# The first batch's attention rows: kept in SBUF and turned around by the tensor engine, in place of a store to DRAM and gathers

## The chip, the cores and the metric

The kernel runs on one core of one Trainium2 chip. The metric is the device time of one launch in microseconds (us). The kernel before took 1281.42 us, the median of three runs (1279.94 to 1284.14). The host only lays out inputs and puts the output rows back in order.

## The reference

Eight batches of eight heads of block-causal attention (576 positions, head size 64, blocks of 64), then, per batch, the real part of a two-dimensional Fourier transform, a normalization and a feed-forward layer.

```python
scores = scale * np.matmul(q, k.transpose(0, 1, 3, 2))
scores = np.where(block_i >= block_j, scores, -1000000000.0)
attn = softmax(scores)
x = np.matmul(attn, v)           # then (batch, position, 8 heads * 64)
mixed = np.real(fft(fft(x, axis=1), axis=2))
u = x + mixed
un = (u - mean(u)) / np.sqrt(var(u) + 1e-06)
out = u + np.maximum(un @ w_ch1, 0.0) @ w_ch2
```

## The kernel before

`tile_attn_fourier_ffn` writes one instruction stream for the whole launch. Pieces of work are `Step` objects in lanes: loading and preparing a head, the row maxima, the scores, the values, and the Fourier transform of a batch. A second list, `feeds`, holds the feed-forward steps of finished row tiles; they are the filler between attention steps. A third, `sides`, holds the weight loads and their conversion. The loop at line 1068 keeps estimated queues of the engines and picks the next step; `AHEAD` (line 36) says how far a side step may be queued on an engine. Each engine then runs in that order (`Ordered`, `keep_in_program_order`), so a changed step or cost can move instructions on every engine.

Attention, per head: `max_part` (row maxima, "lead" matmuls), `shift`, `scores` (pairs of "rest" and "lead" matmuls, exponentials on ScalarE as `ph` and `p`, the small part `pl` on GpSimd), `values` (45 "av" matmuls). At the end of `values`, VectorE divides: `den`, `rec`, and one multiplication of 128x320 into `x`. After every second head, two SP DMAs store the pair's columns of `x` to the DRAM tile `xd`.

When the last head of a batch is stored, `mirror` (line 603) reads back: 256 lower rows into `LL`, 33 middle rows into `X2` (both by SP), and, in reversed row order, the upper rows into `UU` and `U2` by three indirect GpSimd DMAs with the table `rows`. `folded` (line 625) adds and subtracts lower and upper rows on VectorE ("tmp", then the split "fs"); `stage1` and `stage2` are the Fourier matmuls ("dft"), with split results "zc", "zs", "ZT"; `stage2_cos` makes "dif" and "add" on VectorE and adds them to `u` on GpSimd. `normalized_steps` then makes mean and variance, `un`, its transposition ("ident,un"), and `uh`/`ul`, which open a feed of two row tiles.

A feed has two parts: `first` ("h<-uh,W" and "h<-ul,W", 192 matmuls of 256 columns) and `second` ("acc<-W,gh", "acc<-W,gl", 192 of 512 columns). Feed 1 does all of `first` and then all of `second`. Its weights are made meanwhile: `weight_single` has three VectorE instructions on a 128x1024 tile ("W<-W"), one ScalarE square, then a scale per matrix (`weight_scale`, "wst<-ps") and `weight_parts` on ScalarE, GpSimd and VectorE. `second` waits for the scale of the second matrix.

```python
sync.dma_start(LL, xd[0:256].rearrange("(c p) d -> p c d", p=P))
sync.dma_start(X[2], xd[256:289])
for dst, i in ((U[0], 0), (U[1], 1), (U2[0:32], 2)):
    gpsimd.indirect_dma_start(dst, None, xd, bass.IndirectOffsetOnAxis(ap=rows[0:dst.shape[0], i:i + 1], axis=0))
```

Of the kernel before, what the change touches and what calls it, by code (L numbers as in the profile page):

```python
# [9 lines left out]
F32 = mybir.dt.float32  # L10
# [4 lines left out]
ALU = mybir.AluOpType  # L15
# [4 lines left out]
B, H, S, D = 8, 8, 576, 64  # L20
DM = H * D
FF = 4 * DM
P = 128
# [9 lines left out]

HOP = 0.25
MARGIN = 0.3
AHEAD = (3.0, 6.0)
FREE = 0.5

TABLES = (1, 2, 4, 5)
# [161 lines left out]
def tile_attn_fourier_ffn(  # L201
# [5 lines left out]
    work = pool("work")  # L207
# [4 lines left out]
    def ps_tile():  # L212
        return ps[current].tile([P, 512], F32, name=current)

    def mm(*args, **kw):
        return tc.keep_in_program_order(nc.tensor.matmul(*args, **kw))  # L216
# [4 lines left out]
    vector, scalar, gpsimd, sync = (Ordered(tc, x) for x in (nc.vector, nc.scalar, nc.gpsimd, nc.sync))  # L221


    ident = const.tile([P, P], F32, name="ident")
# [59 lines left out]
    def ready(step):  # L284
        r = max((done[x] for x in step.after), default=0.0)
        return max(r, min(rings[x][0] for x in lent)) if step.bank else r
# [13 lines left out]
    def issue(step):  # L300
        nonlocal current, now
        t = max(now, ready(step))
        if step.cost:
            give(t)
        if step.cost:
            now = t = t + step.cost
            for x in queues.values():
                x.forget(now)
        free = None
        starts = []  # L310
        for engine, cost in step.chain:
            if engine == "B":
                free = t + HOP
            elif engine == "L":
                t = t + cost
            elif engine in scratch:

                if cost:
                    t = max(t, scratch[engine][0] - HOP)
                else:  # L320
                    scratch[engine] = sorted(scratch[engine][1:] + [t + HOP])
            else:
                t = book(engine, t + HOP, cost)
                if engine != "M":
                    starts.append(t - cost)
        t += HOP
        if step.key is not None:
            done[step.key] = t
        if step.bank:
            current = min(lent, key=lambda x: rings[x][0])  # L330
            rings[current] = rings[current][1:] + [t if free is None else free]
        parts = step.emit()
        if parts is None:
            return
        if step.cost:
            next(parts, None)
        for at in starts:
            pending.append((at, len(pending) + 1000000 * issued[0], parts))
        issued[0] += 1
# [179 lines left out]
    xs = {}  # L519
    avs = {}  # L520

    def values(h, at):
        g, hh = divmod(h, 2)
        b, n = divmod(h, H)
        vh, vl = VH[g % 2], VL[g % 2]
        if at == 0:
            avs[h] = ps_av.tile([P, 5, D + 1], F32, name="av")
        av = avs[h]
        c = CHUNKS[at]
        tile_, col = ((0, 0), (1, 0), (2, 0), (2, 320), (1, 448))[c]  # L530
        ph, pl = probs[h, tile_]
        for j in range(c, 5):

            lo = col + P * (j - c) - (64 if j == 4 else 0)
            for i, (lhs, rhs, w) in enumerate((
                (ph, vh[:, c, hh], D + 1), (ph, vl[:, c, hh], D), (pl, vh[:, c, hh], D + 1)
            )):
                mm(
                    av[:, j, 0:w], lhs[:, lo:lo + P], rhs, start=(at == 0 and j == 0 and i == 0),
                    stop=(at == 4 and i == 2), skip_group_check=True,  # L540
                )
        if at < 4:
            return
        yield
        del avs[h]
        if n == 0:
            xs[b] = dram.tile([S, DM], F32, name="xd")
        if hh == 0:
            xs["pair"] = work.tile([P, 5, 2, D], F32, name="x", bufs=1)
        xd, x = xs[b], xs["pair"]  # L550
        den, sc = DEN[h % 2], pairs[g]
        eps = 1e-9 * 2.0 ** PSHIFT
        vector.tensor_scalar(den, av[:, :, D], eps, sc, op0=ALU.add, op1=ALU.mult)
        rec = work.tile([P, 5], F32, name="rec", bufs=2)
        vector.reciprocal(rec, den)
        vector.tensor_tensor(
            x[:, :, hh], av[:, :, 0:D], rec.unsqueeze(2).to_broadcast([P, 5, D]), op=ALU.mult
        )
        yield
        if hh == 1:  # L560
            ds = slice(D * (n - 1), D * (n + 1))
            sync.dma_start(
                xd[0:512, ds].rearrange("(c p) d -> p c d", p=P), x[:, 0:4].rearrange("p c h d -> p c (h d)")
            )
            sync.dma_start(xd[512:576, ds], x[64:128, 4].rearrange("p h d -> p (h d)"))
            yield
# [20 lines left out]
    def value_lane():  # L587
        for h in range(B * H):
            for n, c in enumerate(CHUNKS):
                yield Step(  # L590
                    lambda n=n: values(h, n), 0.09 * (5 - c), ("D0.95",) + (("Q1.2",) if h % 2 else ()) if n == 4 else (),
                    (("S", h, (0, 1, 1, 2, 2)[n]), ("N", h // 2)) + ((("V", h - 1, 4),) if h else ()) + ((("d", h // H - 3, "u"),) if n == 4 and h >= 3 * H else ()),
                    ("V", h, n), place=h + 0.5,
                )


    def utile():
        return work.tile([P, 2, DM], F32, name="u", bufs=5)

    def fourier_steps(b):  # L600
        U, X, low, up = [], [], [], []

        def mirror():
            xd = xs.pop(b)
            LL, UU = utile(), utile()
            U.extend((UU[:, 0], UU[:, 1], work.tile([97, DM], F32, name="U2", bufs=1)))
            X.extend((LL[:, 0], LL[:, 1], work.tile([33, DM], F32, name="X2", bufs=1)))
            low.extend(X[0:2])
            up.extend(U[0:2])
            if b % 2 == 0:  # L610
                lefts.append(work.tile([P, DM], F32, name="left", bufs=2))
            U2 = U[2]
# [3 lines that stand above are left out]
                gpsimd.indirect_dma_start(  # L616
                    dst, None, xd, bass.IndirectOffsetOnAxis(ap=rows[0:dst.shape[0], i:i + 1], axis=0)
                )
            gpsimd.memset(U[0][0:1], 0.0)
            gpsimd.memset(U2[32:33], 0.0)  # L620
            yield
# [90 lines left out]
        def stage2_cos(c):  # L712
# [27 lines left out]

        D_ = lambda *a: ("d", b) + a
        place = H * (b + 0.9)
        yield Step(
            mirror, 0.0, ("P3", "L2.5"), (("V", H * b + H - 1, 4),) + ((("F", feed_number(b - 2, 1)),) if b > 1 else ()), D_("u"),
            place=place,
        )
        def folds(name, op, width):
            for c in (2, 0, 1):
                yield Step(
                    lambda c=c: folded(op, width, name, c), 0.0, ("t1",) + (("X1.6", "A1.2", "X0.9") if c == 2 else ("X1.12", "A0.41", "X0.43")) + ("t",), (D_("u"),),  # L750
                    D_("f" + name) if c == 1 else None, place=place,
                )
# [14 lines left out]
        for c in (2, 0, 1):  # L767
# [3 lines left out]
                place=place,  # L771
# [9 lines left out]
    lefts = []  # L781
# [48 lines left out]
    def feed_number(b, i):  # L830

        return 2 * b + 1 + b // 4 if i == 2 else 2 * b + 1 + (b + 1) // 4 + i
# [227 lines left out]
    def transform_lane():  # L1060
        for b in range(B):
            yield from fourier_steps(b)

    lanes = [table_lane(), head_lane(), prepare_lane(), v_lane(), max_lane(), score_lane(), value_lane(), transform_lane()]
    heads = [next(x) for x in lanes]
    weights, filler = [load_lane(), *(weight_lane(w) for w in range(2))], None
    sides = [next(x) for x in weights]
    while True:
# [13 lines left out]
        for w, side in enumerate(sides):  # L1082
# [86 lines left out]
```

## Time and profile before

| | |
|---|---|
| median of three runs | 1281.42 us (1279.94 to 1284.14) |
| the profiled execution's own time | 1277.07 us |
| its span, first to last instruction | 1275.3 us |
| mean granted TensorE clock | 0.947 of full speed |
| busy share: PE, VectorE, ScalarE, GpSimd | 93%, 55%, 43%, 41% |

The span is what the trace covers; some 1.8 us of the execution lie outside it. PE is TensorE's matmul queue, PEld its weight loads, DVE is VectorE, ACT ScalarE, POOL GpSimd, and SP the queue that issues most DMAs. A busy share is a mean over stages: this kernel has an opening stage without filler and a long stage with it, and they have to be read apart.

### The profile page before, as it was taken

Reading aid. Unit: us, or ns where it says so; the run is one execution under the profiler, and the core shown is the slowest. Engines: PE = TensorE matmul, PEld = TensorE weight load, DVE = VectorE, ACT = ScalarE, POOL = GpSimd, SP = SyncE. Lnnn points to the kernel's source line nnn. Section 1 sums busy time; section 2 is a strip of 40 time slices with the busy share of each in tenths; the row PEclk is TensorE's granted clock in tenths of the full one; section 3 lists DMA queues with packets and bytes.
Section 4 is the critical chain, followed back from the end, with each engine's and each line's share of the span. In section 5 each row is a group of like instructions: output and inputs, shape, how many; then the busy total and the mean of one; then the engine's idle time right before and its main releaser. Section 6 shows DMA issues by size and latency. Waiting matters only on the chain.

```text
span 1275.3 us, 25121 instructions
## 1 busy us (share of the span) xinstructions
PE 1181.1 (93%) x10068; PEld 892.9 (70%) x10068; DVE 703.5 (55%) x1433; ACT 548.7 (43%) x1137; POOL 523.6 (41%) x593
## 2 busy tenths in 40 slices
PE   5772598999799999999999999999999999999998
PEld 5672376677677777777777777777777667766665
DVE  6787777756747574664546573557445414422211
ACT  5655647554444555534645545454443112111110
POOL 4664944454643654563534644446441400300000
PEclk9655688999899999999999999999999999999999
DMA  7674242342223233232323232413220100000000
GB/s 210 201 243 156 80 140 70 87 111 52 74 71 109 62 81 86 79 75 54 93 75 95 65 90 68 111 51 87 77 74 10 40 19 19 21 17 1 17 17 17
DMA packets 56371, 99.07 MB, mean 78 GB/s; under 512 B 7757, under 2 KB 26653, under 8 KB 56256
## 3 DMA queue, kind: packets, MB, share of 16 engines
q1 hardware_dynamic: 49152, 73.16, 21.2%
q10 hardware_dynamic: 4384, 16.78, 4.0%
q0 software_dynamic: 2720, 7.54, 2.1%
q8 instruction: 79, 1.29, 0.4%
q14 instruction: 36, 0.29, 0.1%
HBM read 58.46 MB, written 18.87 MB: 61 GB/s over the span
## 4 chain that ended last, share of the span: by engine, by line
PE 80%; DVE 10%; POOL 3%; issue 3%; DMA 2%; ACT 1%; SPq 0%; DVEq 0%; POOLq 0%; ACTq 0%
PE acc L216 28%; PE h L216 27%; PE ps L216 17%; PE av L216 6%; DVE W L194 2%; DVE M L194 2%; DVE tmp L194 2%; PE ps L219 2%; POOL u L194 1%; DMA lead<-mt 1%; DVE VL L194 1%; POOL W L194 1%; POOL pl L194 1%; DVE rest L194 1%; POOL ag L194 0%
## 5 line engine op out<-in xcount | busy, mean ns | idle before, releaser
L216 PE MATMUL h<-uh,W 128*128 128x256 f16 x2304 | 431.4, 275 | 2.7 <-DVE M L194 2.3
L194 POOL TENSOR_TENSOR pl<-p,ph 128x288 f16<-128x288 f32 (+1 forms) x256 | 253.7, 1002 | 355.6 <-ACT p L194 167.8
L216 PEld LDWEIGHTS <-W 128*128 128x128 f16 x3456 | 325.8, 99 | 64.9 <-issue 6.3
L216 PE MATMUL acc<-W,gh 128*128 128x512 f16 x1104 | 329.8, 380 | 0.0
L216 PE MATMUL h<-ul,W 128*128 128x256 f16 x1152 | 315.8, 274 | 0.0
L194 DVE TENSOR_REDUCE M<-ps 128x1 f32<-128x448 f32 (+3 forms) x292 | 131.9, 484 | 181.3 <-PE ps L216 180.5
L194 ACT ACTIVATE gh<-h 128x512 f16<-128x512 f32 x138 | 82.3, 597 | 305.1 <-PE h L216 302.3
L216 PE MATMUL ps<-lead 72*128 72x64 f32 (+9 forms) x700 | 201.3, 346 | 9.2 <-ACT lead L194 6.8
L216 PE MATMUL acc<-W,gl 128*128 128x512 f16 x552 | 209.2, 379 | 0.0
L194 DVE SCALAR_TENSOR_TENSOR gl<-h,gh 128x512 f16<-128x512 f32 x138 | 94.6, 687 | 200.9 <-ACT gh L194 200.8
L194 ACT ACTIVATE ph<-ps 128x512 f16<-128x512 f32 (+1 forms) x233 | 117.5, 506 | 146.9 <-PE ps L216 144.3
L216 PEld LDWEIGHTS <-gh 128*128 128x128 f16 x1104 | 96.7, 98 | 80.1 <-issue 4.7
L216 PEld LDWEIGHTS ps<-lead 72*128 72x128 f32 (+1 forms) x700 | 128.0, 202 | 18.3 <-ACT lead L194 6.8
L216 PEld LDWEIGHTS <-ph 128*128 128x128 f16 x1920 | 113.5, 104 | 31.1 <-ACT left L194 4.9
L216 PE MATMUL ps<-rest 128*128 128x320 f32 (+3 forms) x350 | 124.0, 361 | 1.4 <-ACT p L194 0.8
L216 PE MATMUL av<-VH,ph 128*128 128x65 f16 x960 | 118.1, 203 | 6.1 <-DVE x L194 6.1
L194 ACT ACTIVATE p<-ps 128x512 f32<-128x512 f32 (+1 forms) x233 | 117.2, 505 | 4.3 <-POOL pl L194 2.8
L216 PE MATMUL av<-VH,pl 128*128 128x65 f16 x960 | 116.6, 201 | 1.8 <-POOL pl L194 1.4
L216 PE MATMUL av<-VL,ph 128*128 128x64 f16 x960 | 117.2, 201 | 0.0
L194 POOL TENSOR_TENSOR rest<-raw,lead 64x576 fp32r<-64x576 f32 x64 | 96.9, 1514 | 15.1 <-ACT lead L194 9.5
L216 PEld LDWEIGHTS <-gl 128*128 128x128 f16 x552 | 54.0, 98 | 66.2 <-DVE gl L194 1.7
L216 PEld LDWEIGHTS <-pl 128*128 128x128 f16 x960 | 94.8, 103 | 2.7 <-POOL pl L194 2.5
(169 smaller groups left out, 1435.4 us busy)
## 6 DMA issues: line engine op xcount, KB each, us to landing
raw<-in_qk_dram SPq DMA_DIRECT2D x64, 288.0 KB
rest<-lead SPq DMA_DIRECT2D x128, 144.0 KB
W<-in_moe_w_ch_dram ACTq DMA_DIRECT2D x14, 1024.0 KB
V<-in_v_dram SPq DMA_DIRECT2D x32, 320.0 KB
xd<-x SPq DMA_DIRECT2D x32, 256.0 KB
out_dram<-u SPq DMA_DIRECT2D x32, 256.0 KB
u<-xd SPq DMA_DIRECT2D x8, 512.0 KB
u<-in_moe_w_ch_dram ACTq DMA_DIRECT2D x4, 512.0 KB
```

Source lines behind the costliest of these rows:

```text
L194: x = f(*args, **kw)
L216: return tc.keep_in_program_order(nc.tensor.matmul(*args, **kw))
L219: return tc.keep_in_program_order(nc.tensor.transpose(*args, **kw))
```

## The change

For batch 0 alone, the rows no longer pass through DRAM. `first_rows` takes the tiles `LL`, `X2`, `UU`, `U2` at head 0 and builds `flip`, a reversed identity with zeros on both sides. The division of each head writes three pieces: chunks 3 and 4 into a slot of `x`, chunk 2 into `X2`, chunks 0 and 1 into `LL`. After each pair of heads, `turned` multiplies with slices of `flip` (five fp32 matmuls into one PSUM bank) and ScalarE copies the result into `UU` and `U2`. `known` only hands the tiles on, at no instruction. The eight stores, two loads, three gathers and two GpSimd memsets of batch 0 are gone. `AHEAD` goes from (3.0, 6.0) to (2.75, 3.0). The other seven batches are as before.

```diff
-AHEAD = (3.0, 6.0)
+AHEAD = (2.75, 3.0)
...
+        if b == 0:
+
+            LL, X2, _, _ = xs[0]
+            hs = slice(D * n, D * (n + 1))
+            at = n // 2 % 2 * 2
+            for dst, lo, hi in ((x[:, at:at + 2, hh], 3, 5), (X2[:, hs].unsqueeze(1), 2, 3), (LL[:, :, hs], 0, 2)):
+                vector.tensor_tensor(
+                    dst, av[:, lo:hi, 0:D], rec[:, lo:hi].unsqueeze(2).to_broadcast([P, hi - lo, D]), op=ALU.mult
+                )
+            yield
+            return
...
+    flip = work.tile([P, DM], F32, name="un", bufs=2)
+    def first_rows():
+        LL, UU = utile(), utile()
+        U2 = work.tile([97, DM], F32, name="U2", bufs=1)
+        X2 = work.tile([P, DM], F32, name="X2", bufs=1)
+        xs[0] = LL, X2, UU, U2
+        vector.memset(flip[:, 0:65], 0.0)
+        vector.memset(flip[:, 193:256], 0.0)
+        vector.tensor_copy(flip[:, 65:193], ident[:, ::-1])
+        vector.memset(U2[32:33], 0.0)
+    def turned(n):
+        LL, X2, UU, U2 = xs[0]
+        x = xs["pair"]
+        ds = slice(2 * D * n, 2 * D * (n + 1))
+        t = ps_tile()
+        at = (slice(0, P), slice(P, 2 * P), slice(2 * P, 3 * P))
+        last = [x[:, n % 2 * 2 + c].rearrange("p h d -> p (h d)") for c in range(2)]
+        mm(t[:, at[0]], flip[:, 0:P], last[0], start=True, stop=False, skip_group_check=True)
+        mm(t[:, at[0]], flip[64:P, 64:64 + P], last[1][64:P], start=False, stop=False, skip_group_check=True)
+        mm(t[:, at[1]], flip[:, P:2 * P], last[0], start=False, stop=False, skip_group_check=True)
+        mm(t[:, at[1]], flip[:, 0:P], X2[:, ds], start=False, stop=False, skip_group_check=True)
+        mm(t[0:32, at[2]], flip[:, P:P + 32], X2[:, ds], start=False, stop=True, skip_group_check=True)
+        yield
+        scalar.copy(UU[:, :, ds], t[:, 0:2 * P].rearrange("p (c x) -> p c x", c=2))
+        scalar.copy(U2[0:32, ds], t[0:32, at[2]])
+        yield
...
-        yield Step(
-            mirror, 0.0, ("P3", "L2.5"), (("V", H * b + H - 1, 4),) + ((("F", feed_number(b - 2, 1)),) if b > 1 else ()), D_("u"),
-            place=place,
-        )
+        if b == 0:
+            for n in range(H // 2):
+                yield Step(
+                    lambda n=n: turned(n), 1.3, ("A0.7", "B"), (("V", 2 * n + 1, 4),), D_("t", n), True, place=2 * n + (1.6 if n == 3 else 2.6),
+                )
+            yield Step(known, 0.0, (), tuple(D_("t", n) for n in range(H // 2)), D_("u"), place=place)
```

The planner's order changes with it. On VectorE, at the end of head 7 (division `den`, `rec`, `x`) and the first folds, the order was:

```order
L194 TENSOR_SCALAR DEN_93<-av,vacc 128x5
L194 RECIPROCAL rec<-DEN_93 128x5
L194 TENSOR_TENSOR x<-av,rec 128x5x64
L194 COPY wst<-ps 128x1
L194 TENSOR_SCALAR pw<-wst 128x1
L194 TENSOR_SCALAR wst<-pw 128x1 x2
L194 TENSOR_SCALAR W<-W 128x1024
L194 SCALAR_TENSOR_TENSOR W<-W 128x1024 x2
L194 TENSOR_SCALAR W<-W 128x1024
L194 SCALAR_TENSOR_TENSOR W<-W 128x1024 x2
L194 TENSOR_TENSOR tmp<-X_1246,U_1245 33x512
L194 TENSOR_TENSOR tmp<-tmp 33x255
```

Now it is (`X_355` is `X2`, `u` is `LL` or `UU`):

```order
L194 TENSOR_SCALAR DEN_93<-av,vacc 128x5
L194 RECIPROCAL rec<-DEN_93 128x5
L194 TENSOR_TENSOR x<-av,rec 128x2x64
L194 TENSOR_TENSOR X_355<-av,rec 128x64
L194 TENSOR_TENSOR u<-av,rec 128x2x64
L194 TENSOR_SCALAR W<-W 128x1024
L194 SCALAR_TENSOR_TENSOR W<-W 128x1024 x2
L194 TENSOR_TENSOR tmp<-X_355,U_354 33x512
L194 TENSOR_TENSOR tmp<-tmp 33x255
L194 TENSOR_SCALAR W<-W 128x1024
L194 SCALAR_TENSOR_TENSOR W<-W 128x1024
L194 TENSOR_TENSOR fs_1301<-tmp,fs_1301 32x257
```

One group of three weight instructions stands ahead of the first fold, where there were two; two of the second group stand behind that fold, and the third, further on, ahead of "ZT".

Later on VectorE, between the two "zs" results of the first transform stage and the first "dif", the order was:

```order
L194 TENSOR_TENSOR zs_1370<-ps,zs_1370 128x288
L194 TENSOR_SCALAR W<-W 128x1024
L194 SCALAR_TENSOR_TENSOR W<-W 128x1024 x2
L194 TENSOR_TENSOR zs_1373<-h,zs_1373 128x288
L194 TENSOR_SCALAR W<-W 128x1024
L194 SCALAR_TENSOR_TENSOR W<-W 128x1024 x2
L194 TENSOR_TENSOR dif<-ps,bs 33x258
```

Now it is:

```order
L194 SCALAR_TENSOR_TENSOR W<-W 128x1024
L194 TENSOR_TENSOR ZT<-h,ZT 2x290
L194 TENSOR_TENSOR zs_1399<-ps,zs_1399 128x288
L194 TENSOR_TENSOR zs_1401<-acc,zs_1401 128x288
L194 TENSOR_SCALAR W<-W 128x1024
L194 SCALAR_TENSOR_TENSOR W<-W 128x1024 x2
L194 TENSOR_TENSOR dif<-ps,bs 33x258
```

The weight group that stood between the two "zs" is gone from there.

On TensorE, behind the transform of batch 0, the order was this, and then 45 "av" matmuls of head 8, six "lead" and four score matmuls of head 9 before the feed's first "h<-uh,W":

```order
L216 MATMUL acc<-lead_84 128x320
L216 MATMUL ps<-lead_84 128x448
L216 MATMUL acc<-lead_84 128x512
L219 MATMUL acc<-ident,M_91 5x128
L219 MATMUL acc<-ident,un 128x128 x8
L216 MATMUL h<-vacc,ones 128x1
```

Now the transposition stands right behind the transform, ahead of the twelve score matmuls of head 8; the last four of these, three "lead" of head 9 and the start of the feed are:

```order
L216 MATMUL h<-rest_89 128x320
L216 MATMUL h<-lead_86 128x320
L216 MATMUL h<-rest_89 128x192
L216 MATMUL h<-lead_86 128x192
L216 MATMUL ps<-lead_84 128x64 x2
L216 MATMUL ps<-lead_84 128x192
L216 LDWEIGHTS W
L216 MATMUL h<-uh,W 128x256
```

The values of head 8 and the maxima and scores of head 9 have moved behind the start of the feed.

## Rows read from the trace of the kernel before

**Rows 1.** The page's busy times of the engines over the whole span.
```profile
PE 1181.1 (93%) x10068; PEld 892.9 (70%) x10068; DVE 703.5 (55%) x1433; ACT 548.7 (43%) x1137; POOL 523.6 (41%) x593
```
**Rows 2.** Stages: window, PE, PEld, DVE, ACT, POOL busy, granted clock, DMA share, GB/s.
```profile
0.00:98.00 98.00, 67.65 (x531) 60.14 (x531) 75.97 (x154) 55.99 (x114) 55.30 (x60) 0.72 0.74 220
98.00:164.20 66.20, 29.24 (x156) 22.64 (x157) 51.02 (x73) 40.81 (x78) 48.90 (x54) 0.60 0.37 118
164.20:215.00 50.80, 42.47 (x392) 36.14 (x391) 36.21 (x70) 28.00 (x58) 20.91 (x20) 0.82 0.37 100
...
340.00:1276.00 936.00, 927.44 (x7976) 689.77 (x7975) 455.81 (x967) 358.66 (x752) 337.66 (x395) 1.00 0.21 58
```
**Rows 3.** The chain of waits from 95 us: start, us, what.
```profile
97.37 0.49 DVE x L194
...
97.89 3.44 DMA xd<-x
...
101.39 3.54 DMA u<-xd
...
107.66 2.90 DMA U<-xd,rows
...
110.64 0.81 DVE tmp L194
```
**Rows 4.** The timeline of DVE: start, us, instruction, in brackets idle time before it.
```profile
96.89 0.22 DVE L194 TENSOR_SCALAR DEN<-av,vacc 128x5 f32<-128x5 f32 x1
...
98.28 0.68 DVE L194 TENSOR_SCALAR W<-W 128x1024 int32<-128x1024 int32 x1
99.00 3.32 DVE L194 SCALAR_TENSOR_TENSOR W<-W 128x1024 int32<-128x1024 int32 x2
...
136.45 0.41 DVE L194 TENSOR_TENSOR dif<-ps,bs 33x258 f32<-33x258 f32 x1
...
209.30 0.16 DVE L194 COPY wst<-ps 128x1 f32<-128x1 f32 x1 [2.14 <-PE ps L216]
```
**Rows 5.** Waits of PE from 98 to 164 us: us in total, times, longest.
```profile
PE ps L216 <- DVE zs L194: 3.5, 1, 3.5
```
**Rows 6.** The timeline of PE.
```profile
95.66 0.38 PE L216 MATMUL ps<-wst,ones 128*128 128x1 f32 x2 [2.90 <-DVE wst L194]
...
133.62 0.42 PE L216 MATMUL ps<-dft,ZT 34*33 34x258 f32 x1
...
154.91 1.12 PE L219 MATMUL acc<-ident,un 128*128 128x128 f32 x4 [2.91 <-DVE un L194]
...
157.99 0.21 PE L216 MATMUL av<-VH,ph 128*128 128x65 f16 x1
...
164.23 0.37 PE L216 MATMUL h<-uh,W 128*128 128x256 f16 x1 [0.32 <-ACT p L194]
...
215.00 0.61 PE L216 MATMUL acc<-W,gh 128*128 128x512 f16 x2
```
**Rows 7.** Waits of DVE up to 98 us.
```profile
DVE x L194 <- DMA xd<-x: 1.9, 1, 1.9
```
**Rows 8.** The chain of waits from 215 us: start, us, what, how many.
```profile
217.30 1.96 PE acc L216 x9
...
220.88 0.47 PE av L216 x15
...
238.74 0.83 PE ps L216 x6
...
252.31 2.64 PE h L216 x24
```
**Rows 9.** Groups of batch 0's folds (DVE) and additions (POOL): ns min/median/max, starts.
```profile
L194 DVE TENSOR_TENSOR tmp<-u x4: 673/680/3245, 112.7 to 123.9; 128x512 f32<-128x512 f32 x4
...
L194 POOL TENSOR_TENSOR u<-u,add x4: 714/1210/1704, 142.1 to 148.1; 128x255 f32<-128x255 f32 x2, 128x257 f32<-128x257 f32 x2
```
**Rows 10.** Waits of PE from 250 to 400 us.
```profile
PE ps L219 <- DVE DEN L194: 4.9, 1, 4.9
```

More of the change, by code (lines that the diff above doesn't have):

```diff
@@ L545, in values @@
         del avs[h]
-        if n == 0:
+        if n == 0 and b == 0:
+            first_rows()
+        elif n == 0:
             xs[b] = dram.tile([S, DM], F32, name="xd")
-        if hh == 0:
+        if hh == 0 and (b or n == 0):
             xs["pair"] = work.tile([P, 5, 2, D], F32, name="x", bufs=1)
-        xd, x = xs[b], xs["pair"]
+        x = xs["pair"]
         den, sc = DEN[h % 2], pairs[g]
@@ L555, in values @@
         vector.reciprocal(rec, den)
+        if b == 0:
[8 more added lines that the diff above has]
+            return
+        xd = xs[b]
         vector.tensor_tensor(
@@ L590, in value_lane @@
                 yield Step(
-                    lambda n=n: values(h, n), 0.09 * (5 - c), ("D0.95",) + (("Q1.2",) if h % 2 else ()) if n == 4 else (),
-                    (("S", h, (0, 1, 1, 2, 2)[n]), ("N", h // 2)) + ((("V", h - 1, 4),) if h else ()) + ((("d", h // H - 3, "u"),) if n == 4 and h >= 3 * H else ()),
+                    lambda n=n: values(h, n), 0.09 * (5 - c), (("D1.3",) if h < H else ("D0.95", "Q1.2") if h % 2 else ("D0.95",)) if n == 4 else (),
+                    (("S", h, (0, 1, 1, 2, 2)[n]), ("N", h // 2)) + ((("V", h - 1, 4),) if h else ()) + ((("d", h // H - 3, "u"),) if n == 4 and h >= 3 * H else ()) + ((("d", 0, "t", h // 2 - 2),) if n == 4 and 2 < h < H and h % 2 == 0 else ()),
                     ("V", h, n), place=h + 0.5,
@@ L598, in utile, with known @@
         return work.tile([P, 2, DM], F32, name="u", bufs=5)
+    flip = work.tile([P, DM], F32, name="un", bufs=2)
[10 more added lines that the diff above has]
+        LL, X2, UU, U2 = xs[0]
+        x = xs["pair"]
+        ds = slice(2 * D * n, 2 * D * (n + 1))
[11 more added lines that the diff above has]
+        yield
     def fourier_steps(b):
         U, X, low, up = [], [], [], []
+        def known():
+            LL, X2, UU, U2 = xs.pop(b)
+            U.extend((UU[:, 0], UU[:, 1], U2))
+            X.extend((LL[:, 0], LL[:, 1], X2))
+            low.extend(X[0:2])
+            up.extend(U[0:2])
+            lefts.append(work.tile([P, DM], F32, name="left", bufs=2))
         def mirror():
@@ L742, in fourier_steps @@
         place = H * (b + 0.9)
-        yield Step(
-            mirror, 0.0, ("P3", "L2.5"), (("V", H * b + H - 1, 4),) + ((("F", feed_number(b - 2, 1)),) if b > 1 else ()), D_("u"),
-            place=place,
-        )
+        if b == 0:
[4 more added lines that the diff above has]
+            yield Step(known, 0.0, (), tuple(D_("t", n) for n in range(H // 2)), D_("u"), place=place)
+        else:
+            yield Step(
+                mirror, 0.0, ("P3", "L2.5"), (("V", H * b + H - 1, 4),) + ((("F", feed_number(b - 2, 1)),) if b > 1 else ()), D_("u"),
+                place=place,
+            )
         def folds(name, op, width):
```

## The prediction

> **What bounds the kernel now.** I read the busy times first: PE is busy 1181.1 of 1275.3 us, no other engine over 55% [rows 1]. A mean over stages hides where the other 94 us are, so I read the stages next. From 340 us to the end PE is busy 927.4 of 936 us at the full clock: there nothing but matmul work counts. In the first 215 us PE is idle 30.4 us (to 98 us), 37.0 us (98 to 164 us) and 8.3 us (164 to 215 us), at granted clocks of 0.72, 0.60 and 0.82, that is partly at the lower of the two levels [rows 2]. So a change in the opening is worth the time by which the saturated state comes earlier, as long as the work that is done by then is the same. I mark its beginning by the first matmul of the second feed-forward part, "acc<-W,gh", at 215.0 us [rows 6].
>
> What holds the middle stage is read from the chain of waits: head 7's division ends at 97.86 us, the store to DRAM takes 3.44 us, the load back 3.54 us, two gathers are issued, and the third lands 2.90 us after its issue; the first fold starts at 110.64 us [rows 3]. That is a gap of 12.8 us, after which the transform, the normalization and 6.2 us of attention follow until the feed begins at 164.23 us [rows 6].
>
> **The change, part by part.** The sum is made against the profiled execution, 1277.1 us; the median of the runs shown is 4.3 us above it, and I add that at the end.
>
> *A. The handover of head 7's rows.* Removed: the 12.8 us. Added: a division in three pieces. The one of 128x320 takes 0.49 us and the instruction of 128x5 ahead of it 0.22 [rows 3, 4], so two more instructions cost at most 0.44 us; I take 0.35. Then one weight group stands ahead of the first fold, 0.68 + 3.32 = 4.0 us [rows 4]. Beside it, TensorE turns the last pair. A plain fp32 matmul of this width is not in the trace. Below it lies a transposition, four in 1.12 us, 0.28 apiece; above it I count two of these for each, because the one plain fp32 matmul on "ones" shows as two instructions [rows 6]: 1.4 to 2.8 us for five. I take 2.1, as the data type is that of the upper row and the width that of the lower one. With two ScalarE copies, taken at VectorE's 0.41 us for 258 columns [rows 4], and hops this is 3 to 4 us, about as long as the weight group, which covers it. If the copies wait behind other work on ScalarE, some 6.8 us stand in the gap. A saves 12.8 - 4.4 = 8.4 us at best, 6.0 at worst; I take **8.0**.
>
> *B. First fold to first feed matmul, 53.6 us before* (110.64 to 164.23). The order shows four things leave this stretch. The weight group between the two "zs" goes: PE waited 3.5 us for it [rows 5]. The group ahead of "dif" no longer ends last: PE had finished its operand at 134.04 and "dif" began at 136.45, 2.4 us [rows 4, 6]. Five maximum reductions and a "rest" ahead of the mean and variance go, at the 1.7 us by which they stood in the way (my estimate: half of eight instructions of 0.4 us). Head 8's values and head 9's maxima and scores go behind the feed's start: PE worked on them from 157.99 to 164.23, 6.2 us [rows 6]. Added: three weight instructions among the folds, 0.68 + 3.32 = 4.0 us [rows 4], and the wait until ScalarE and GpSimd have emptied the PSUM banks of head 8's scores, which the feed needs; I take 4, within 0 and the 6.2 us that the attention work there took before. Sum 13.8 - 8.0 = 5.8: **B saves 5.8**; 9.8 if the last wait is hidden, and a loss of 1.2 if what is told below as the lock decides.
>
> *C. Feed start to 215.0 us, 50.8 us before.* Counted in the order up to the first "acc<-W,gh", PE has done nearly the same work: 15 "av" and one score pair fewer, one "lead" more. So what left B comes back here: 12 "lead", 30 "av" and one score pair. At full clock 15 "av" take 0.47 and six matmuls with these operands 0.83 us [rows 8]: 12 x 0.14 + 0.94 + 0.28 = **2.9 us added**. Between 0, since PE is idle 8.3 us there [rows 2], and 4.5 at the lower clock.
>
> *D. The head stage, 98 us before.* Added on VectorE: 8 x 0.35 = 2.8 us, and once four small instructions for `flip` and `U2`, some 0.8 by the 0.22 us of a short instruction [rows 4]: 3.6 us. Added on PE: three turnings, 6.3 us. In the stage both have room (22.0 and 30.4 us idle [rows 2]), but they release one another. No turning waits: each stands in PE's queue behind "av" work that itself needed the division it reads. Behind it queue the next head's scores, and ScalarE waits for those. Removed: six of the eight stores on SP's queue, which "rest" copies and "mt" no longer queue behind, and one wait of the division for a store, 1.9 us [rows 7]. I take half of VectorE's 3.6, a third of PE's 6.3, less half of the 1.9: **3 us added**; the ends are -1.9 and 8 x 0.44 + 0.8 + 8.4 = 12.7.
>
> *E. Work not yet done at the marker*: 0.47 + 0.28 - 0.14 = **0.6 us added** later.
>
> *F. The next seam.* Near 335 us PE waits 4.9 us [rows 10]: the first two feeds are used up before batch 1's is ready. In the new order batch 1's transform begins with 24 + 9 more feed matmuls left, 2.64 + 1.96 = 4.6 us of filler [rows 8]. **2 us saved**, between 0 and 4.6.
>
> The fourth turning falls into PE's idle middle stage, the GpSimd queue loses the gathers and two memsets, and `AHEAD` works only through the order already counted. Sum: -8.0 - 5.8 + 2.9 + 3 + 0.6 - 2 = -9.3 us, 1277.1 - 9.3 = 1267.8, and with 4.3 added **1272 us**. Bounds together: -24 and +13 us.
>
> **The rivals.**
>
> *More is gained.* The head stage gets shorter by the 1.9 us, the later work hides (C at 0) and the seam closes by 4.6: -8.0 - 5.8 + 0 - 1.9 + 0.6 - 4.6 = -19.7, so 1262 us. For it: VectorE's waits on DMAs disappear; against it: VectorE is busy 76.0 of 98 us in that stage [rows 2].
>
> *The lock.* [...] The fold "tmp<-u" took 0.68 us in the middle and once 3.2; GpSimd's "u<-u,add" 0.71 to 1.70, median 1.21 [rows 9]. More weight groups now stand beside the additions. If nine more of the twelve additions go from 0.71 to 1.21 and one more fold to 3.2, B loses 4.5 + 2.6, some 7 us: -2.3, so 1279 us, no change. [...]
>
> *The head stage pays in full.* D at 12.7 in place of 3: +0.4, so 1282 us, no change. Against it: 22 us of idle VectorE.
>
> *The second weight matrix holds the marker, and the kernel is slower.* "acc<-W,gh" needs the scale copied at 209.30 us, for which VectorE waited 2.1 us [rows 4]. Ten weight groups still have to run between head 7 and that scale, each behind a load, ScalarE's square and the planner's place. If this chain is already the bound, A, B, C and F vanish, and VectorE's 3.6 us, PE's 2.1 and E's 0.6 remain: 1281.4 + 6.3 = 1287.7. It decides if the copy comes later than 209.3 us although the feed starts earlier. For it: PE is idle just before the marker; against it: VectorE is busy only 87.2 of the 117 us from 98 to 215 [rows 2].
>
> That the change doesn't do what it says is excluded: in the new order batch 0 has no stores, loads or gathers of rows.
>
> **How the numbers follow.** A measurement here tells a difference of about 0.3% from none, 3.8 us: 1277.6 to 1285.3 is no change. My forecast has 0.46, more gain 0.18, the lock 0.12, the head stage 0.10, the weights 0.09, and 0.05 is left for other shifts of the order. Faster: 0.46 + 0.18, a quarter of the lock, and 0.04 from the head stage and the rest: 0.71. Slower: the weights and a little of the rest, 0.10. No change: 0.19. The range from 1260 to 1282 us takes in all of the forecast and the lock, most of the larger gain and half of the head stage; it leaves out the slower case and the far end of the gain.
>
> **What would show it.** After the change the first fold should come some 5 us after head 7's division (12.8 before), the first feed matmul at 164.2 - 13.8 + 3, near 153 us, the scale of the second matrix copied before 203, and "acc<-W,gh" near 207. The division of head 7 should end near 101 us. Gathers of batch 0 must be missing. I am wrong in A if the fold waits for ScalarE's copies, in B if "dif" or "un" waits long for GpSimd, in C if PE sits idle ahead of "acc<-W,gh" by more than the 8 us before, in D if head 7 ends before 96 or after 106, in F if the wait near 330 us grows. If the marker comes early and the time does not fall by as much, the gain was given back later.

## The result and the profile after

The changed kernel took 1287.0 us, the median of 19 runs, beside 1281.0 for the kernel before on the same chip: ratio 1.0043, 95% interval 1.0031 to 1.0055. It is slower, where 1272 us and faster had been forecast, and the time lies outside the range of 1260 to 1282 us. The profiled execution took 1282.31 us (1277.07 before), its span is 1280.5 us (1275.3).

The stages of the changed kernel, to be laid beside [rows 2]: window, PE, PEld, DVE, ACT, POOL busy, granted clock, DMA share, GB/s.

```profile
0.00:98.00 98.00, 68.27 (x561) 58.25 (x561) 76.16 (x172) 57.60 (x122) 56.71 (x60) 0.76 0.70 205
98.00:164.20 66.20, 26.14 (x131) 20.40 (x132) 55.19 (x72) 40.14 (x76) 43.48 (x50) 0.64 0.26 89
164.20:215.00 50.80, 44.78 (x428) 37.56 (x425) 40.30 (x81) 27.98 (x59) 19.98 (x17) 0.87 0.41 114
...
340.00:1276.00 936.00, 926.66 (x7919) 687.60 (x7917) 455.66 (x958) 354.51 (x746) 335.40 (x389) 1.00 0.21 57
```

Up to 215 us PE is idle as long as before: 29.7 + 40.1 + 6.0 = 75.8 us, where it was 75.6. In the middle stage it is idle 3 us more, although the gathers are gone. The lower of the clock's levels is 0.50: of the 170 windows of 2 us up to 340 us, 97 show 1.00 and 59 show 0.50 in the kernel before, 106 and 49 in the change; the rest lie between. Behind 340 us it is idle more too: 9.3 us up to 1276 us, in a kernel that runs on to 1280.5, where the 8.6 us before included the last 0.7 us, after that kernel had ended.

The timeline of VectorE, as in [rows 4]: the division in three pieces, the first fold, the three "dif" of batch 0 with the weight group between them, "un", and the copy of the second scale.

```profile
98.48 0.29 DVE L194 TENSOR_TENSOR x<-av,rec 128x128 f32<-128x128 f32 x1
98.69 0.21 DVE L194 TENSOR_TENSOR X<-av,rec 128x64 f32<-128x64 f32 x1
98.81 0.28 DVE L194 TENSOR_TENSOR u<-av,rec 128x128 f32<-128x128 f32 x1
99.01 1.44 DVE L194 TENSOR_SCALAR W<-W 128x1024 int32<-128x1024 int32 x1
100.48 3.32 DVE L194 SCALAR_TENSOR_TENSOR W<-W 128x1024 int32<-128x1024 int32 x2
103.72 0.68 DVE L194 TENSOR_TENSOR tmp<-X,U 33x512 f32<-33x512 f32 x1
...
127.99 0.41 DVE L194 TENSOR_TENSOR dif<-ps,bs 33x258 f32<-33x258 f32 x1
...
131.90 0.43 DVE L194 TENSOR_TENSOR dif<-h,bs 128x258 f32<-128x258 f32 x1 [3.17 <-POOL U L194]
...
132.58 4.83 DVE L194 TENSOR_SCALAR W<-W 128x1024 int32<-128x1024 int32 x1
...
139.85 0.42 DVE L194 TENSOR_TENSOR dif<-ps,bs 128x258 f32<-128x258 f32 x1
...
148.82 0.55 DVE L194 TENSOR_SCALAR un<-u,ag 128x512 f32<-128x512 f32 x1 [2.24 <-POOL ag L194]
...
205.21 0.15 DVE L194 COPY wst<-ps 128x1 f32<-128x1 f32 x1
```

The first fold comes 4.6 us after the division's end, not 12.8. Then the weight instruction at 132.58 takes 4.83 us in place of 0.68. GpSimd's timeline beside it:

```profile
131.84 1.14 POOL L194 TENSOR_TENSOR W<-p,W 128x512 f16<-128x512 f32 x1
132.95 0.72 POOL L194 TENSOR_TENSOR u<-u,dif 128x257 f32<-128x257 f32 x1
133.63 1.40 POOL L194 TENSOR_TENSOR u<-u,add 128x255 f32<-128x255 f32 x2
135.00 0.72 POOL L194 TENSOR_TENSOR u<-u,dif 128x255 f32<-128x255 f32 x1
...
135.72 1.14 POOL L194 TENSOR_TENSOR W<-p,W 128x512 f16<-128x512 f32 x1
```

GpSimd works without a gap until 136.86 us; the VectorE instruction ends 0.55 us later, about its own length. It was held for the whole row of GpSimd instructions, six `tensor_tensor` and a memset, not for one of them. By what mechanism, no run here shows.

The timeline of PE, as in [rows 6]: the last turning, the transposition of "un", the first scores of head 8, the first feed matmul, the marker.

```profile
98.82 1.32 PE L216 MATMUL ps<-x,un 128*128 128x128 f32 x6 [1.32 <-DVE x L194]
99.98 0.72 PE L216 MATMUL ps<-X,un 128*128 128x128 f32 x4
...
149.42 1.11 PE L219 MATMUL acc<-ident,un 128*128 128x128 f32 x4 [20.12 <-DVE un L194]
...
152.07 0.59 PE L216 MATMUL ps<-rest 128*128 128x288 f32 x1
...
159.83 0.37 PE L216 MATMUL h<-uh,W 128*128 128x256 f16 x1 [2.28 <-ACT p L194]
...
212.49 0.61 PE L216 MATMUL acc<-W,gh 128*128 128x512 f16 x2
```

The marker is reached 2.5 us before its old time, where 8 had been forecast, yet the span is 5.2 us longer: behind the marker 1068.0 us pass, before 1060.3. Most of that is one place, in batch 3's folds. First VectorE, then GpSimd, then PE there:

```profile
518.58 3.37 DVE L194 TENSOR_TENSOR tmp<-u 128x512 f32<-128x512 f32 x1
```
```profile
517.97 1.12 POOL L194 DMA_DIRECT2D fs<-U  x2 [2.12 <-ACT U L194]
519.06 2.33 POOL L194 TENSOR_TENSOR pl<-p,ph 128x512 f16<-128x512 f32 x2
```
```profile
525.03 0.77 PE L216 MATMUL ps<-lead 72*128 72x512 f32 x1 [3.66 <-DVE M L194]
```

The fold is held as in [rows 9], until 0.56 us behind the second "pl". Behind it on VectorE stand the maxima "M", for which PE waits 3.66 us. Then PE runs at half its clock, 0.50 for 6 us (window, PE busy, granted clock):

```profile
521.00:525.00 4.00, 0.36 (x3) 0.94 0.28 65
525.00:531.00 6.00, 5.97 (x31) 0.50 0.20 49
```

That is 3.7 us of waiting and some 3 us of half-speed work: 6.7 us, beside 7.7 us lost behind the marker. It is not the whole account, since other waits there became shorter or longer. The stretch from the marker to the end, in the kernel before and in the change (window, PE busy, instructions left for PE, granted clock):

```profile
215.00:1275.30 1060.30, 1041.77 (x8990) 1.00 0.22 61
```
```profile
212.49:1280.50 1068.01, 1046.97 (x9006) 0.99 0.22 61
```

PE is idle there 18.5 us before and 21.0 us after, 2.5 us more, and busy 5.2 us longer with nearly the same work.

### The profile page after: what moved, and what is told of

The parts are those of the page before. It is cut to its first block, busy times and chain, and to the rows that moved or that the text cites. A ratio compares the mean times of both kernels' runs of the same rounds, so it can differ in the third digit from the quotient of the medians.

```text
span 1280.5 us, 25210 instructions
## 1 busy us (share of the span) xinstructions
PE 1183.6 (92%) x10108; PEld 891.1 (70%) x10108; DVE 713.2 (56%) x1453; ACT 549.1 (43%) x1145; POOL 522.5 (41%) x588
## 4 chain that ended last, share of the span: by engine, by line
PE 80%; DVE 9%; POOL 3%; DMA 3%; issue 2%; ACT 2%; SPq 0%; DVEq 0%; ACTq 0%; POOLq 0%
PE acc L216 28%; PE h L216 28%; PE ps L216 17%; PE av L216 6%; DVE W L194 2%; DVE tmp L194 2%; PE ps L219 1%; DVE M L194 1%; DMA lead<-mt 1%; DMA W<-in_moe_w_ch_dram 1%; POOL pl L194 1%; DVE un L194 1%; POOL W L194 1%; POOL u L194 1%; DVE VL L194 1%
## 5 line engine op out<-in xcount | busy, mean ns | idle before, releaser
L194 POOL TENSOR_TENSOR pl<-p,ph 128x288 f16<-128x288 f32 (+1 forms) x256 | 258.1, 1021 | 350.0 <-ACT p L194 189.6
L194 DVE TENSOR_REDUCE M<-ps 128x1 f32<-128x512 f32 (+3 forms) x296 | 134.0, 486 | 171.4 <-PE ps L216 168.4
L216 PEld LDWEIGHTS ps<-lead 73*128 73x128 f32 (+1 forms) x701 | 125.7, 199 | 28.7 <-ACT lead L194 8.2
L216 PE MATMUL ps<-rest 128*128 128x288 f32 (+1 forms) x348 | 123.0, 361 | 3.0 <-DVE M L194 2.1
```

What stands on the lines that cost most here:

```text
L194: x = f(*args, **kw)
```

## The experiments

Theory, called the lock theory in the expectations: the handover gained what was forecast, and what was lost again are VectorE instructions held while GpSimd works, in the places to which the new order brought them. Rivals: `AHEAD` is at fault (the planner theory); the second weight matrix holds the marker; the turnings cost PE time in the head stage; work was put behind the feed that would have filled idle time. Ratios are to the kernel before, run on the same chip, with 95% intervals.

**The change with the old AHEAD.**

```diff
-AHEAD = (2.75, 3.0)
+AHEAD = (3.0, 6.0)
```

> The change with AHEAD at its old value (3.0, 6.0). Planner theory (the loss comes from AHEAD, the rows on the chip gain what was predicted): 1270 to 1276 us, faster than the kernel before by 5 us or more. Lock theory (VectorE is held while GpSimd works through queued instructions, in the middle stage and once near 520 us): which instructions meet is a matter of the order, so no gain is owed to AHEAD itself; 1280 to 1290 us, and the time follows the number of VectorE instructions that last over 3 us in place of some 0.7, at some 3 us each in the middle stage.

1274.6 us, ratio 0.9969 (0.9957 to 0.9981): 4.0 us faster than before, and 0.7% faster than the change. The planner theory holds in size: at the old value the loss is not there. The forecast "no gain is owed to AHEAD" falls. How it costs that, the next runs tell. The lock theory's count fails in the middle stage: this trace has a held weight instruction there too, longer than the change's, and yet the run is the faster one.

```profile
139.12 5.95 DVE L194 TENSOR_SCALAR W<-W 128x1024 int32<-128x1024 int32 x1
```

It has no held fold, in batch 0 or later, and PE does not wait at the seam near 335 us (window 300 to 340 us, PE busy throughout):

```profile
300.00:340.00 40.00, 40.00 (x376) 31.23 (x373) 26.32 (x60) 19.25 (x42) 23.99 (x32) 1.00 0.28 76
```

**The kernel before with the new AHEAD.**

```diff
-AHEAD = (3.0, 6.0)
+AHEAD = (2.75, 3.0)
```

> The kernel before with AHEAD at (2.75, 3.0), nothing else; the order moves only behind the feed's start, near 164 us. Planner theory: the new values cost the change its gain, so here they cost as much, 1287 to 1292 us. Lock theory: within 3 us of the kernel before, 1278 to 1284 us, unless a new wait of PE of over 3 us appears behind 215 us.

1277.6 us, ratio 0.9985 (0.9975 to 0.9995). The value is not bad by itself; it costs only in the order that it draws together with the new steps.

**One weight group pushed out of the additions.**

```diff
-(("scale", 0), ('V', 7, 4)) if w else ()), ("WS", x),
+(("scale", 0), ('V', 7, 4)) if w else ()) + ((("d", 0, "u", 1),) if x == 11 else ()), ("WS", x),
```

> The change, with one more condition: the weight group that stands between the additions of batch 0 and takes 4.83 + 2.48 us on VectorE waits for the last of them. Lock theory: the last 'dif' starts near 133 in place of 139.9 us, 'un' near 144 in place of 148.8, the first feed matmul near 155 in place of 159.8, the time 1282 to 1284 us, 3 to 5 below the change. Theory that the second weight matrix holds the marker: the scale is copied later than 205.2 us by up to the 5 us of the group that is pushed back, 'acc<-W,gh' does not start before 212.5 us, and the time is that of the change, 1286 to 1290 us.

1292.4 us, ratio 1.0102 (1.0087 to 1.0116), slower than the change by 0.6%. The group was held all the same, now behind the last "dif", for the seven GpSimd instructions that follow there:

```profile
139.60 7.01 DVE L194 TENSOR_SCALAR W<-W 128x1024 int32<-128x1024 int32 x1
```

"un" was no earlier (151.0 us; in this execution head 7 had ended 3.2 us later than in the change's profile), the second scale was copied at 215.3 and the marker fell to 220.1 us. So the run doesn't show what an open tail is worth. It does bear out the rival of the weights in one direction: if the groups are put off, the marker goes with them.

**Batch 3's two small transfers issued on SP.** The orders of PE and VectorE are the same as in the change.

```diff
-gpsimd.dma_start(t[96 + a:97 + a, 0:width], rr[a])
+(sync if b == 3 else gpsimd).dma_start(t[96 + a:97 + a, 0:width].bitcast(F32), rr[a].bitcast(F32))
```

> The change, with two small transfers of batch 3 (fs from U, 1 KB each) issued on SP in place of GpSimd, where they wait for ScalarE and hold two 'pl' instructions behind them; the order of PE and VectorE is the same. Lock theory: the fold of 3.37 us at 518.6 takes 0.7 us, PE's wait of 3.66 us at 525 us goes, and with it the stretch of 6.8 us at half the clock: 6 us less than the change, 1280 to 1282 us. Rival (the wait only shows work that is late anyway): the wait is put off to a later place, 1285 to 1289 us.

1278.8 us, ratio 1.0003 (0.9992 to 1.0014): 0.4% or 5 us below the change. The fold (VectorE), PE's wait and the clock (window, PE busy, clock) are now:

```profile
518.02 1.65 DVE L194 TENSOR_TENSOR tmp<-u 128x512 f32<-128x512 f32 x1
```
```profile
522.75 0.47 PE L216 MATMUL ps<-lead 72*128 72x512 f32 x1 [2.50 <-DVE M L194]
```
```profile
515.00:525.00 10.00, 7.50 (x76) 1.00 0.22 50
525.00:535.00 10.00, 10.00 (x84) 1.00 0.11 32
```

The wait is shorter by 1.2 us only, but the clock does not fall behind it. Between the divisions of heads 30 and 48 the change's profile loses 6.4 us on this one, 4.8 of them between heads 31 and 33, around the fold. The held fold near 520 us is thus shown to cost about 5 us. (The fold of 3.32 us at 282 us is gone too in this profile, though nothing was edited there; a little of the 5 us may be its.)

The two kernels have the same order up to the marker, yet this profile reaches it 2.7 us later than the change's and no earlier than the kernel before. Behind it, with exactly the work that the change has left there, 1059.1 us pass, where it was 1068.0:

```profile
215.19 0.61 PE L216 MATMUL acc<-W,gh 128*128 128x512 f16 x2
```
```profile
215.19:1274.30 1059.11, 1040.82 (x9006) 1.00 0.22 61
```

**Head 8 may begin earlier.** In the change PE idles 20.1 us ahead of "un" with the scores of head 8 queued behind it. The planner starts them only when all 16 tiles of the first weight matrix are made.

```diff
-or ('w', 15) in done)
+or ('w', 12) in done)
```

> The change with its AHEAD, but the planner may begin head 8 when 13 of the 16 tiles of the first weight matrix are made, not all 16: the scores of head 8 and the maxima of head 9 then stand ahead of the transposition of 'un' on PE. Theory of the idle middle stage (work put behind the feed is not saved, it leaves a stage in which PE has nothing else): PE's wait of 20.1 us ahead of the transposition gets some 6 us of this work, the first feed matmul comes at about the same time with that work done, and the time falls by 3 to 6 us against the change, to 1280 to 1283 us. Lock theory alone (only the held VectorE instructions cost): 1285 to 1289 us, as long as the fold near 518 us is held.

1285.2 us, ratio 1.0047 (1.0034 to 1.0060), as the change. The scores did move, and from 100 to 165 us PE is busy 31.4 us in place of 25.8. But PE then waits 2.32 us at 235 us and falls to half its clock:

```profile
235.00:243.00 8.00, 7.94 (x40) 0.57 0.24 68
```

and the fold near 520 us is held as before (3.36 us). Filling 5.6 us of the idle middle stage brought no gain, so the theory of the idle middle stage is not borne out. The run can't rule it out, because its order differs from the change's up to the middle of the program, with the new wait at 235 us in it.

**Both repairs together** (the two edits above).

> The change with its AHEAD and both edits that were tried alone: head 8 may begin at 13 tiles of the first weight matrix, and batch 3's two small transfers are issued on SP. If the two repairs add up (5 us from the fold near 520 us, 5.6 us of PE's idle time in the middle stage, of which the first run kept nothing since PE fell to half the clock near 214 and 236 us): 1279 to 1281 us, no better than the transfers alone; below 1276 us the half clock near 236 us was an accident of that run, above 1283 us the fold was not what the transfers mended.

1282.1 us, ratio 1.0030 (1.0019 to 1.0041): better than the earlier start alone, worse than the transfers alone. Half the clock near 235 us was there again (granted clock 0.79 from 235 to 243 us), so it was no accident of one run.

**Each turning twice**, at the old `AHEAD` (the run to compare with is the first, 0.9969).

```diff
+        for _ in range(2):
-        mm(t[:, at[0]], flip[:, 0:P], last[0], start=True, stop=False, skip_group_check=True)
+            mm(t[:, at[0]], flip[:, 0:P], last[0], start=True, stop=False, skip_group_check=True)
...
```

> The change at the old AHEAD (3.0, 6.0), each of the four turnings issued twice on PE, with the same result; the order is otherwise that of the run with the old AHEAD. The theory of the prediction's term D (a third of the turning's PE time reaches the end of the head stage): four more turnings of 2.0 to 2.4 us, 8 to 10 us of PE time, cost 2 to 4 us, so 1276 to 1279 us. Rival (PE's time in the head stage counts in full, since PE's queue releases ScalarE and VectorE): 8 to 10 us more, 1282 to 1285 us. Other rival (wholly hidden): 1274 to 1275 us.

1286.3 us, ratio 1.0070 (1.0056 to 1.0084), 1% or 12.9 us more than with single turnings: more than even the rival. One doubled turning on PE, at half the clock (0.50 from 40 to 47 us):

```profile
40.31 2.08 PE L216 MATMUL acc<-x,un 128*128 128x128 f32 x6
42.17 1.20 PE L216 MATMUL acc<-X,un 128*128 128x128 f32 x4
43.30 2.24 PE L216 MATMUL acc<-x,un 128*128 128x128 f32 x6
45.34 1.20 PE L216 MATMUL acc<-X,un 128*128 128x128 f32 x4
```

The rival's price was too low. Three of the four added turnings took 3.2 us like the second one here, and one, mostly at the full clock, took 1.9: 11.5 us in all, about what the run lost.

**The turnings of six heads left out**, again at the old `AHEAD`.

```diff
+        if n < 3:
+            mm(t[:, 0:1], flip[:, 0:P], last[0][:, 0:1], start=True, stop=False, skip_group_check=True)
+            mm(t[:, 1:2], flip[:, 0:P], X2[:, 2 * D * n:2 * D * n + 1], start=False, stop=True, skip_group_check=True)
...
```

> The change at the old AHEAD, where the turnings of pairs 0 to 2 are cut to two matmuls of one column each (ScalarE copies that column as widely as before), so the upper rows of six heads hold other numbers; the orders of VectorE and ScalarE are the same. Theory that PE's time in the head stage counts in full (as the doubled turnings showed, 12.9 us for four): head 7 ends 5 to 8 us earlier, near 95 us, and the time falls by 5 to 8 us, to 1267 to 1270 us. The prediction's third: 2 to 3 us, 1272 to 1273 us. Rival (the doubled turnings were dear only because they pushed something over a threshold, the single ones are hidden): 1274 to 1275 us.

1273.1 us, ratio 0.9954 (0.9940 to 0.9967), 2 us less, which the intervals do not tell from nothing. The three runs' "rec" of head 7 stands at 110.48 (twice), 102.23 (once) and 101.73 us (left out), one profile each. So the doubled turnings cost in full and the single ones little: the room in the head stage seems to be used up by the first. That the single turnings cost in full falls; between a third of PE's time, as forecast, and nothing this run does not decide.

**The turnings half a head later**, at the old `AHEAD`.

```diff
-place=2 * n + (1.6 if n == 3 else 2.6),
+place=2 * n + (1.6 if n == 3 else 3.1),
```

> The change at the old AHEAD, with the turnings of pairs 0 to 2 placed half a head later in the planner's order, behind more of the next head's work. If the turning costs in full wherever it stands in the head stage (PE's queue is what bounds it): 1273 to 1277 us, as the run with the old AHEAD. If it costs because the scores of the next head queue behind it and ScalarE waits for those: some 3 to 6 us less, 1269 to 1272 us.

1282.8 us, ratio 1.0028 (1.0015 to 1.0041), 0.6% slower than unmoved, against both expectations. Head 7's "rec" came earlier (98.86 us), but this order has the held fold (3.36 us at 520.0) and PE's 3.65 us behind it again.

**All batches' small transfers on SP**, with the rows on the chip at the old `AHEAD`, and in the kernel before.

> The change at the old AHEAD, with the two small transfers of every batch (fs from U) issued on SP in place of GpSimd. Lock theory: no fold over 3 us is left in the later batches, and GpSimd no longer waits for ScalarE with 'pl' behind it; that run had no held fold anyway, so 1271 to 1275 us, 0 to 3 below the run with the old AHEAD. Rival (SP's queue, which loads and stores, now waits for VectorE and holds the loads behind): 1277 us or more.

1274.5 us, ratio 0.9968 (0.9960 to 0.9977): nothing gained where no fold was held, and nothing lost.

> The kernel before with the same two transfers on SP in every batch, nothing else. Lock theory: its two folds of 3.25 and 3.36 us (at 116 and 285 us) take 0.7, the one at 116 us lies on the chain to the feed, so 2 to 4 us below the kernel before, 1275 to 1277 us. Rival (what is released ends at the next wait): within 1 us of the kernel before.

1281.5 us, ratio 1.0020 (1.0011 to 1.0029): slower, not 2 to 4 us faster, and outside the rival's 1 us too. The two held folds are gone, but now the weight instruction behind the last "dif" is held, 5.96 us where it had taken 0.95. A hold that was taken away in one place turned up in the next; that this is what cost the 2.4 us is not shown.

**Other values of AHEAD**, to see what the order alone does.

> The rows on the chip with AHEAD at (3.5, 6.0), a third value that neither kernel has. If what AHEAD does is only to draw another order, of which some hold VectorE or leave PE without work: anywhere between 1272 and 1288 us, with PE's waits of over 1 us behind 215 us to match. If 2.75 is bad because side steps (the making of weights) are held back too long, so that head 8 may begin only late: 3.5 is as good as 3.0 or better, 1270 to 1276 us, with the scores of head 8 ahead of the transposition of 'un'.

1286.2 us, ratio 1.0064 (1.0044 to 1.0083), with PE waiting 4.38 us at 255 us. The order alone can do this; that a larger value is as good falls.

> The rows on the chip with AHEAD at (3.25, 6.0); the kernel before has the same order at 3.0, 3.25 and 3.5, so its time stands for all three. If the rows on the chip are worth some 4 us by themselves (0.9969 at 3.0) and 3.5 was a bad draw: 0.994 to 0.999 of the kernel before. If their worth is within the spread that the order alone makes: anywhere from 0.995 to 1.007; the sign at 3.25 then says little, and the mean over the values of AHEAD is near 1.

1279.9 us, ratio 1.0004 (0.9995 to 1.0014): above the 0.994 to 0.999 of a worth of 4 us, within the spread.

> The rows on the chip with AHEAD at (2.5, 6.0). Theory that a low AHEAD is bad for the rows on the chip (side steps held back): 1.004 or more, as at 2.75. Theory that AHEAD only draws an order: anywhere from 0.995 to 1.007, and over 1.003 only if the trace shows PE waiting over 2 us behind 215 us or a held fold of over 3 us with PE waiting for it.

1284.1 us, ratio 1.0037 (1.0025 to 1.0049), with a fold held 3.36 us at 403.9 and a wait of PE of 4.25 us at 274.7.

> The kernel before with AHEAD at (2.5, 6.0). If the order alone spreads times by 0.5% whatever the rows do: 0.998 to 1.007. Its order behind the first batches is nearly that of the change, so the lock theory expects the held fold of 3.3 us near 515 us, PE's wait of some 3.7 us behind it and 4 to 6 us lost there: 1.002 to 1.006 of the kernel before. If the loss in the change came from the rows on the chip, it is not here: 0.997 to 1.001.

1289.8 us, ratio 1.0087 (1.0074 to 1.0100), above all three expectations. All five pairs (the second value of `AHEAD` is 6.0, at 2.75 it is 3.0; at 3.25 and 3.5 the kernel before keeps its order):

| AHEAD | through DRAM | rows on the chip | quotient |
|---|---|---|---|
| 2.5 | 1.0087 | 1.0037 | 0.995 |
| 2.75 | 0.9985 | 1.0043 | 1.006 |
| 3.0 | 1 | 0.9969 | 0.997 |
| 3.25 | 1 | 1.0004 | 1.000 |
| 3.5 | 1 | 1.0064 | 1.006 |

The order alone spreads either design by about 1%, as much as the change was to bring, and the quotient's sign changes from value to value. So what the rows on the chip are worth by themselves these pairs do not show. One comparison goes further. Behind some 240 us the order of the last run is that of the change, on every engine, with the rows in DRAM. It has the held fold (VectorE) and the wait (PE):

```profile
524.89 3.36 DVE L194 TENSOR_TENSOR tmp<-u 128x512 f32<-128x512 f32 x1
```
```profile
531.33 0.47 PE L216 MATMUL ps<-lead 72*128 72x512 f32 x1 [3.86 <-DVE M L194]
```

So that loss belongs to the order, not to the rows on the chip. The division of head 20 there, and then in the change:

```profile
349.50 0.19 DVE L194 RECIPROCAL rec<-DEN 128x5 f32<-128x5 f32 x1
```
```profile
342.19 0.19 DVE L194 RECIPROCAL rec<-DEN 128x5 f32<-128x5 f32 x1
```

There the change is 7.3 us ahead. Of that 3.0 us are left at the end of the profiles; in the ratios it is 1.0043 / 1.0087 = 0.9956, 5.6 us. This is not the worth of the rows alone, because ahead of 240 us the two orders differ, among others in the weight groups on VectorE. Nor is the last run's loss (0.87%, 11.1 us) the price of the order that the two share. Its marker and the stretch behind it:

```profile
219.90 0.61 PE L216 MATMUL acc<-W,gh 128*128 128x512 f16 x2
```
```profile
219.90:1283.50 1063.60, 1044.31 (x9006) 1.00 0.22 61
```

Its span is 8.2 us longer than that of the kernel before. Of these, 4.9 us are lost ahead of the marker, in an order that is neither the kernel before's nor the change's, and only 3.3 behind it.

The fastest design found is the change at the old `AHEAD`, with the small transfers on either queue, 0.3% below the kernel before.

## Why the prediction was wrong

Two steps failed. In the profile the marker comes 2.5 us earlier, where A to D had forecast 7.9; and behind it 7.7 us more pass, where E and F had forecast 1.4 less. Even the 2.5 us are one draw: the run with batch 3's transfers on SP has the same order up to there and reaches the marker at 215.19 us, 0.2 later than the kernel before. Of the loss behind the marker some 5 us are the held fold of batch 3. With that mended, the time is the kernel before's (1.0003): neither the loss nor the forecast gain. What the rows on the chip are worth by themselves stays open, since the quotients at one `AHEAD` run from 0.995 to 1.006.

- **A, the handover: right.** 12.8 - 4.6 = 8.2 us saved, 8.0 forecast. One weight group covers the turning, which ends at 100.7 us, 3 us ahead of the fold. The turning took 1.9 us, forecast 2.1.
- **B, first fold to first feed matmul: wrong in sign.** 56.1 us where it was 53.6: 2.5 lost, 5.8 forecast as saved. From the fold to the second "zs" 0.9 us were saved. The forecast there was 3.5 saved and 4.0 added for the weight instructions among the folds; it did not count that the fold held in the kernel before (3.2 us [rows 9]) would not be held now. Up to the first "dif" 0.6 were saved (forecast 2.4). Between the second and the third "dif" 4.1 were lost, as the held instruction shows, which the sum had at nothing. From there to the statistics 2.2 were saved (1.7 forecast), then 1.1 lost ahead of "un", which waits for GpSimd's "ag". From "un" to the feed 11.0 us pass, where it was 9.9: the step that failed here is "Head 8's values and head 9's maxima and scores go behind the feed's start ... 6.2 us", less 4 for the banks: 2.2 forecast as saved, 1.1 lost. The feed did not come sooner for it, since head 8's scores, at half clock (0.50 from 152 to 158 us), and their exponentials, which the banks wait for, now stand behind "un". Of the 8.3 us between forecast and result, the held instruction and this step are 7.4. What they cost in the end is not shown: the kernel with head 8 ahead of "un" was no faster, but its order differs further on as well.
- **C, feed to marker: right in size**, 1.9 us for 2.9.
- **D, the head stage: right in size.** In the profiled run the division ended 1.2 us later. That was one draw: "rec" of head 7 stands at 98.3, 100.4, 101.5, 101.8 and 100.4 us in the five profiles with this order, at 97.1, 97.2 and 97.6 in three with the rows in DRAM, 3.2 us on the mean, for 3 forecast. How much of it is the turnings is not shown: without six heads' turnings, at the old `AHEAD`, it was 0.5 us earlier, and one order's own draws differ by up to 3.5.
- **E and F: right in size.** At the marker PE has 16 instructions more left than before, 15 of them "av", as E had counted. Near 335 us PE waits 2.2 us, where it was 4.9: 2.7 us, forecast 2.
- **What was missing** is everything behind 340 us. The step that failed is "`AHEAD` works only through the order already counted". The order had been counted up to the seam, and the rest taken as 927 us of busy PE that can't get worse [rows 2]. It got worse by a held fold, of the kind that [rows 9] already showed in the kernel before (a second one, of 3.36 us, stands near 285 us there); batch 3's two small transfers moved to SP give back 5 us.

Of the rivals, **the lock** was right in kind, VectorE held beside GpSimd, in the wrong place and at too low a price. It was put down to additions and one fold in the middle stage, which would have left the time unchanged; there it took 4.1 us on one weight instruction, and outside that stage 5 us. Nine more slow additions the change does not show: three of the twelve took over 1 us in the kernel before (1.18, and two of 3.37 together), and three in the change (1.70, and two of 2.84 together). The hold in the middle stage does not separate slow orders from fast ones: all 13 traces with the rows on the chip have one weight instruction held there, for 4.8 to 7.0 us, the fastest among them, and two of the four with the rows in DRAM. **More gain** did not come. **The weights**, with nearly the right time, did not decide: the second scale was copied at 205.2 us, ahead of 209.3, its own condition. **The head stage in full** did not come either; only the doubled turnings pay in full.

Open is what the held weight instruction costs in the end, since the one run that moved it had it held again in the next place, and why the other orders differ by up to 1%. The runs with an earlier start of head 8 point to PE's waits of some 2 us between 215 and 300 us, some with a spell of half clock behind them, but no run took these away.

## What to carry to other kernels

Where a planner sets the order, a change of the work is also a new draw of the order, and here the draw alone is worth ±0.5%: compare the old and the new work in the same order, or over several settings, before the change itself is judged. Count a new order to the end of the program, and look in it for VectorE instructions that meet a row of GpSimd instructions: one of 0.68 us took 4.83 here beside six. Time won in an opening is kept only if nothing later gives it back. In the saturated stage a wait cost more than itself here: from the end of one of 3.66 us near 525 us on, the clock stood at 0.50 for 6.8 us (524.5 to 531.3).

## What the runs showed that was not expected

- A VectorE instruction was held over a whole row of GpSimd instructions: 4.83 us beside six, 5.95 us beside seven (the change at the old `AHEAD`), 7.01 us beside eight (the group pushed out), each until 0.55 us after the last `tensor_tensor` of GpSimd's row had ended, for an instruction that takes 0.68 us alone.
- In the 17 traces, 116 folds of 128x512 began while GpSimd issued a DMA. The 14 that were held for 3.2 to 3.4 us are among them, each with two more GpSimd instructions directly behind the issue; 101 took at most 0.75 us. So the issue alone does not hold them.
- Near 525 us PE's clock fell to half after a wait of 3.66 us, and not after one of 2.50 us at the same place. But near 235 us, in the run with head 8 earlier, it fell after one of 2.32 us. So the length of the last wait alone does not decide it.
- Five plain fp32 matmuls of up to 128 columns show as ten instructions: 1.9 us for the last turning, at the full clock, 3.2 us for one at half of it.
